# The second mixture's first layer on the byte remainders of the products' operands

## The chip, the cores and the metric

The kernel runs on one core of one Trainium2 chip. The metric is the device time of one execution in microseconds (us); smaller is better. Five engines of the core work side by side, each through its own list of instructions: TensorE (PE, with its weight loads shown apart as PEld), VectorE (DVE), ScalarE (ACT), GpSimd (POOL) and SyncE (SP), which issues most DMAs.

## The reference

Three stages follow each other: linear attention, a mixture of experts with 32 soft slots, and a second mixture that sends every token through all eight experts, weighted by a gate that eight rounds of normalization have balanced. The last takes most of the time, and only it is shown here:

```
def _moe2_ref(x, w_gate, w1, w2):          # x: 2304 tokens x 512
    logits = x @ w_gate
    P = np.exp(logits - logits.max())
    for _ in range(8):
        P /= P.sum(1, keepdims=True) + 1e-09
        P /= P.sum(0, keepdims=True) + 1e-09
        P *= N / E
    for e in range(E):                     # 8 experts, F = 1024
        h = np.maximum(x @ w1[e], 0.0)
        out += P[:, e:e + 1] * (h @ w2[e])
```

The x of this stage is a softmax over 32 slots times the 32 slot outputs, so x @ w1[e] is a product over 32 slots, split in high and low parts to 128 rows.

## The kernel before

**The second mixture.** The 2304 tokens are 9 blocks of 256, and the loop at the end of the kernel runs over 8 experts times 9 blocks, 72 blocks in all, numbered i. For a block, `first_layer(i, n)` makes one half (n = 0, 1) of the hidden layer: four matmuls with a stationary operand of 128x128 from the expert's *stack* (tile st) and the 256 columns of `ct` as moving operand, written to the PSUM tile z. Both operands are fp32r. `ct` holds the softmax over the slots (tiles ct0 to ct3 and ct4, each for two blocks, ct4 for the last block).

**The products.** `hidden(i)` turns z into seven pairs of tiles hh and hl (the rounded high part of a ReLU or of a sum of ReLUs, and what is left of it), made by ACT, DVE and POOL. `product(i, k)`, k = 0 to 6, multiplies a pair by the expert's second-layer weights in a product scheme of seven instead of eight: twelve matmuls each, hh or hl as stationary operand, 256 columns of a weight tile (in the trace w_b or w_t, by the name of its part) as moving one, summed in one of the PSUM tiles x, y, z. `take(i, k)` adds the sum, times the gate, to the output tile xo, on DVE. (Note that z names two PSUM tiles: z<-ct,st is the first layer, z<-w_b a product.)

**The order on PE.** In a block the products come as x (k = 0), z, x; then the first layer of the next block, eight matmuls; then y (k = 3), x, y, x. So 84 product matmuls and 8 of the first layer make a block. All of these have one shape, 128x128 weights and 256 columns. The order is written out by hand; line 51 of the profile is the helper that records every instruction.

**What cuts the stream of matmuls.** When an expert is at its last block, `make_stack` (tile ps) and `spread_stack` (tile pr, from st and the constant rep) make the next expert's stack, between products. In the first expert the normalization of the gate (`sinkhorn`) sums over tokens with a small matmul (tile pcs) once in each of eight rounds, right ahead of the third product.

**Where tiles lie.** Each pool stacks its tiles in the order in which they are first asked for, from its start upward. The pool `const` starts at byte 16512 of each partition and holds, before the change, ct4 (1024 bytes a partition), ident and ones (512 each), wg (128), si (2048), six tiles x0 to x5 (2048 each, later used for ct0 to ct3 and rep) and a tile `pad` of 32 bytes. The pool behind it starts where `const` ends. In the second mixture's pool `cp`, gst (32 bytes) is followed by st (4096) and gm (which takes 32). A byte remainder is the address modulo 512.

Of the kernel before, what the change touches and what calls it, by code (L numbers as in the profile page):

```python
# [7 lines left out]
F32 = mybir.dt.float32  # L8
# [10 lines left out]
E, SPE, FF = 8, 4, 1024  # L19
NS = E * SPE  # L20
KC = DM // 128
# [5 lines left out]
def parts_of(t):  # L27

    out, n = [], t * 128
    while n < (t + 1) * 128:  # L30
        b = n // S
        end = min((b + 1) * S, (t + 1) * 128)
        out.append((b, n - t * 128, end - t * 128))
        n = end
    return out
# [19 lines left out]
def tile_kernel(ctx: ExitStack, tc: tile.TileContext, a):  # L55
# [3 lines left out]
    const = ctx.enter_context(tc.tile_pool(name="const", bufs=1, side="left"))  # L59
# [8 lines left out]
    def load_const(name, shape, pool=None, q=SP):  # L68
        t = (pool or const).tile(shape, F32, name=name, bufs=1)
        q.dma_start(out=t, in_=a[name])  # L70
        return t
# [16 lines left out]
    def w1_unit(name, e, n):  # L88
        return unit_t[name, e, n].rearrange("p (k f) -> p k f", k=2)
# [27 lines left out]
    def load_k(t):  # L117
        x = kp.tile([128, 512], F32, tag="kt", name=f"kt{t}", bufs=4)
        SP.dma_start(out=x, in_=a["kT"][t])
        kt_t[t] = x  # L120

    def load_v(i):
        rows = kp.tile([128, DM], F32, tag="vs", name=f"vs{i}", bufs=2)
        SP.dma_start(out=rows, in_=a["vb"][i])
        x = kp.tile([128, H, XW], F32, tag="vt", name=f"vt{i}", bufs=2)
        G.tensor_copy(out=x[:, :, 0:D], in_=rows.rearrange("p (h d) -> p h d", h=H))
        t, b = VBLOCKS[i]
        parts = parts_of(t)
        for b1, r0, r1 in parts:
            G.memset(x[r0:r1, :, D:XW], float(b1 == b))  # L130
        vt_t[i] = x
# [248 lines left out]
    load_v(0)  # L380
    load_k(2)
    load_v(1)
    ct4 = const.tile([128, 256], F32R, name="ct4", bufs=1)
    ident = load_const("ident", [128, 128])
    ones = load_const("ones", [128, 128])
# [1 line left out]
    for j in range(2):  # L387
        SP.dma_start(out=phi[j * D:(j + 1) * D], in_=a["bd"][j * D:(j + 1) * D, :, j * 96 + D:(j + 1) * 96])
    sel4 = first.tile([128, 128], F32, name="sel4", bufs=1)
    wg = const.tile([128, KC, E], F32, name="wg", bufs=1)  # L390
    lg = early.tile([128, NT, NS], F32, name="lg")
    si = const.tile([128, DM], F32, tag="si", name="si", bufs=1)
    cs = first.tile([128, 2], F32, name="cs")
# [101 lines left out]
            wk = wk_cm.__enter__()  # L495
            attn_units |= {i + 1 + n: (wk, 15 + n) for n in range(7)}
    G = InOrder(tc, G)
    const.tile([128, 8], F32, name="pad", bufs=1)
    while si_steps:
        si_step()  # L500

# [217 lines left out]
    cp = ctx.enter_context(tc.tile_pool(name="cp", bufs=1, side="right", reuse_waits="tile"))  # L719
# [9 lines left out]
    def z_tile(n, name):  # L729
        return pz.tile([128, 1024], F32, tag=f"z{n}", name=name)  # L730

    def make_stack(e):

        ps = z_tile(0, f"ps{e}")[:, 0:256]
        for kc in range(KC):
            w = w1_unit("moe2_w1", e, kc // 2)
            for g in range(4):
                PE.matmul(ps[32 * g:32 * g + 32, :], sot[:, kc, 0:NS], w[:, kc % 2, g * 256:(g + 1) * 256], start=kc == 0, stop=kc == KC - 1)
        for n in range(2):
            unit_t.pop(("moe2_w1", e, n))  # L740

        st = cp.tile([128, FF], F32R, tag="st", name=f"st{e}", bufs=1)
        hl = st[:, FF // 2:].rearrange("p (n f) -> p n f", n=2)
        V.tensor_copy(out=hl[:, 0, :], in_=ps)
        V.tensor_tensor(out=hl[:, 1, :], in0=ps, in1=hl[:, 0, :].bitcast(F32), op=ALU.subtract)
        return st
# [205 lines left out]
    blocks = [(e, blk) for e in range(E) for blk in range(NBLK)]  # L952
    sink = sinkhorn()
    gst = cp.tile([128, E], F32R, name="gst")
    stacks = {0: make_stack(0)}
    gmt = cp.tile([128, 2], F32, name="gm")
    next(sink)
    for k in (4, 5, 6):
        w_part(0, k)
# [108 lines left out]
```

## Time and profile before

| what | us |
|---|---|
| median of 3 runs | 1010.85 |
| the runs | 1010.77 to 1012.33 |
| the profiled execution, its span from first to last instruction | 1010.7 |
| PE busy | 993.3 |
| DVE busy | 691.1 |
| POOL busy | 596.0 |
| ACT busy | 551.8 |

The profiled execution's own time is known as its span; between that and the median of the runs lie 0.15 us. The loop over the 72 blocks begins at about 223 us; what is ahead of it are attention and the first mixture. An engine's busy time is the union of its records. The matmuls' records overlap, each lasting over twice the distance between two starts, so a busy PE says that it never stops, not how quick it is; that is seen from the starts in the timeline.

### The profile page before, as it was taken

What the parts mean: (1) busy time and instruction counts of PE and PEld (TensorE: products, weight loads), DVE (VectorE), ACT (ScalarE), POOL (GpSimd) and SP (SyncE); (2) the same over time, 40 slices, a digit from 0 to 9 for tenths busy, and PEclk for the clock granted to TensorE, in tenths of its full rate; (3) what the DMA queues carried; (4) which work ended last, traced back from release to release, by engine and by line L of the source; (5) the groups of instructions that cost most, each with busy time, mean ns of one, the idle gap of its engine ahead of it and who ended that gap; (6) DMA issues with size and microseconds to landing.
All of it is one profiled execution on the core that took longest, in us unless ns stands there. A gap on an engine that the chain in (4) does not pass through costs nothing.

```text
span 1010.7 us, 27875 instructions
## 1 busy us (share of the span) xinstructions
PE 993.3 (98%) x11638; PEld 938.6 (93%) x11638; DVE 691.1 (68%) x1408; ACT 551.8 (55%) x993; POOL 596.0 (59%) x446
## 2 busy tenths in 40 slices
PE   8999999989999999999999999999999999999998
PEld 7888887449999999999999999999999999999998
DVE  6778876317887677677667676676676677666675
ACT  5665654245566666655565556455555555565442
POOL 2101000475667677858785878578767777686443
PEclk9999999999999999999999999999999999999999
DMA  7767568982003100310031004000400130001111
GB/s 212 227 191 219 162 193 302 350 355 81 1 1 126 43 2 1 126 43 2 2 125 43 2 1 166 3 2 7 161 2 1 65 104 2 1 1 43 43 45 61
DMA packets 25341, 88.84 MB, mean 88 GB/s; under 512 B 3456, under 2 KB 6400, under 8 KB 19328
## 3 DMA queue, kind: packets, MB, share of 16 engines
q1 hardware_dynamic: 19840, 68.05, 19.2%
q10 hardware_dynamic: 5184, 18.88, 6.0%
q8 instruction: 92, 1.51, 0.6%
q14 instruction: 33, 0.27, 0.1%
q0 software_dynamic: 192, 0.13, 0.1%
HBM read 82.33 MB, written 4.72 MB: 86 GB/s over the span
## 4 chain that ended last, share of the span: by engine, by line
PE 95%; DVE 2%; DMA 1%; issue 1%; ACT 1%; DVEq 0%; ACTq 0%
PE x L51 39%; PE y L51 19%; PE z L51 16%; PE kvacc L51 3%; PE num L51 3%; PE pq L51 2%; PE ut L51 2%; PE pk L51 2%; PE ps L51 1%; DMA moe_w<-in_moe_w 1%; PE ph L51 1%; PE po L51 1%; PE lg L51 1%; PE xt L51 1%; PE xl L51 1%
## 5 line engine op out<-in xcount | busy, mean ns | idle before, releaser
L51 POOL TENSOR_TENSOR hl_s<-s,hh_s 128x512 fp32r<-128x512 f32 x286 | 365.5, 1300 | 211.8 <-ACT hh_s L51 192.7
L51 PE MATMUL x<-w_t,hh_s 128*128 128x256 f32 x1152 | 205.4, 278 | 0.0
L51 ACT ACTIVATE hh_s<-s 128x512 fp32r<-128x512 f32 x287 | 175.3, 630 | 52.8 <-DVE s L51 50.4
L51 ACT ACTIVATE r<-z 128x512 f32<-128x512 f32 x143 | 85.6, 599 | 166.5 <-PE z L51 166.0
L51 PEld LDWEIGHTS x<-w_t,hh_s 128*128 128x128 f32 x1152 | 173.7, 188 | 0.8
L51 DVE SCALAR_TENSOR_TENSOR xo<-x,P,xo 128x256 f32<-128x256 f32 x252 | 120.8, 480 | 71.3 <-PE x L51 71.2
L51 ACT ACTIVATE hh_a<-z 128x512 fp32r<-128x512 f32 x216 | 122.3, 600 | 74.4 <-DVE s L51 72.6
L51 PE MATMUL x<-w_t,hl_s 128*128 128x256 f32 x576 | 159.5, 278 | 0.0
L51 DVE SCALAR_TENSOR_TENSOR s<-z,r 128x512 f32<-128x512 f32 x143 | 98.1, 686 | 87.2 <-ACT hh_a L51 82.5
L51 DVE SCALAR_TENSOR_TENSOR hl_a<-z,hh_a 128x512 fp32r<-128x512 f32 x216 | 147.0, 680 | 3.9 <-ACT rt L51 3.9
L51 PEld LDWEIGHTS x<-w_t,hl_s 128*128 128x128 f32 x576 | 108.1, 188 | 0.0
L51 PE MATMUL y<-w_t,hh_s 128*128 128x256 f32 x576 | 103.2, 279 | 0.0
L51 PE MATMUL z<-w_b,hh_a 128*128 128x256 f32 x576 | 102.6, 279 | 0.0
L51 PE MATMUL y<-w_b,hh_s 128*128 128x256 f32 x576 | 102.0, 277 | 0.0
L51 PE MATMUL x<-w_t,hh_a 128*128 128x256 f32 x576 | 102.0, 277 | 0.0
L51 PE MATMUL x<-w_b,hh_a 128*128 128x256 f32 x576 | 101.6, 277 | 0.0
L51 DVE SCALAR_TENSOR_TENSOR s<-z,s 128x512 f32<-128x512 f32 x143 | 97.7, 683 | 3.5 <-POOL hl_s L51 1.3
L51 PEld LDWEIGHTS z<-w_b,hh_a 128*128 128x128 f32 x576 | 86.8, 188 | 2.9 <-issue 2.9
L51 PEld LDWEIGHTS y<-w_t,hh_s 128*128 128x128 f32 x576 | 87.5, 188 | 0.0
L51 PEld LDWEIGHTS x<-w_t,hh_a 128*128 128x128 f32 x576 | 86.9, 188 | 0.1
L51 PEld LDWEIGHTS y<-w_b,hh_s 128*128 128x128 f32 x576 | 86.9, 188 | 0.0
L51 PEld LDWEIGHTS x<-w_b,hh_a 128*128 128x128 f32 x576 | 86.7, 188 | 0.0
(176 smaller groups left out, 1984.5 us busy)
## 6 DMA issues: line engine op xcount, KB each, us to landing
moe_w<-in_moe_w SPq DMA_DIRECT2D x46, 1024.0 KB, 6.0
moe_w<-in_moe_w ACTq DMA_DIRECT2D x36, 512.0 KB, 4.1
vs<-in_vb SPq DMA_DIRECT2D x20, 256.0 KB, 4.0
kt<-in_kT SPq DMA_DIRECT2D x18, 256.0 KB, 3.8
qt<-in_qT SPq DMA_DIRECT2D x18, 256.0 KB, 3.4
out<-xo SPq DMA_DIRECT2D x18, 128.0 KB, 1.7
out<-xo SPq DMA_DIRECT2D x9, 256.0 KB, 2.0
wbd<-in_wbd SPq DMA_DIRECT2D x1, 128.0 KB, 2.7
```

The costliest lines, as they stand in the source:

```text
L51: return lambda *args, **kwargs: self.tc.keep_in_program_order(make(*args, **kwargs))
```

## The change

Tiles are asked for in another order, so that they get other addresses. The built program has the same instructions in the same order on every engine, with the same waits; the order of the instructions shows no difference but the running numbers in the tiles' names.

```
     load_v(1)
+    const.tile([128, 8], F32, name="pad", bufs=1)
+    wg = const.tile([128, KC, E], F32, name="wg", bufs=1)
     ct4 = const.tile([128, 256], F32R, name="ct4", bufs=1)
     ident = load_const("ident", [128, 128])
     ones = load_const("ones", [128, 128])
...
     sel4 = first.tile([128, 128], F32, name="sel4", bufs=1)
-    wg = const.tile([128, KC, E], F32, name="wg", bufs=1)
     lg = early.tile([128, NT, NS], F32, name="lg")
...
     G = InOrder(tc, G)
-    const.tile([128, 8], F32, name="pad", bufs=1)
     while si_steps:
...
     gst = cp.tile([128, E], F32R, name="gst")
+    gmt = cp.tile([128, 2], F32, name="gm")
     stacks = {0: make_stack(0)}
-    gmt = cp.tile([128, 2], F32, name="gm")
     next(sink)
```

What lies ahead of ct4, ident and ones grows by 160 bytes (pad and wg), what lies ahead of si and the x tiles by 32 (pad), what lies ahead of st by 32 (gm). The pools' ends stay where they were, and so do all tiles that aren't listed here:

| tile | its part in matmuls | remainder by 512 before | after |
|---|---|---|---|
| ct0 to ct3 | moving, first layer, blocks 0 to 7 | 256 | 288 |
| ct4 | moving, first layer, block 8 | 128 | 288 |
| st | stationary, first layer; moving for pr | 320 | 352 |
| rep | stationary for pr | 256 | 288 |
| sot | stationary for ps and pgate | 256 | 288 |
| wg | moving for pgate | 128 | 160 |
| ident | moving of all transposes | 128 | 288 |
| ones | stationary for pcs | 128 | 288 |
| si, os, x0 to x5 | in attention and the first mixture | 256 | 288 |
| weight tiles w | moving, all products | 288 | 288 |
| hh, hl | stationary, all products | 352 | 352 |

A matmul of the first layer or of a product steps through its tile by whole multiples of 512 bytes, so that the remainder is that of every such operand.

## Rows read from the trace of the kernel before

**Rows 1.** View of the cores: span us, mean granted TensorE clock.
```profile
core 0: 1010.7 us, clock 1.000
```

**Rows 2.** The page, part 1: busy us, share of the span, instructions.
```profile
PE 993.3 (98%) x11638; PEld 938.6 (93%) x11638; DVE 691.1 (68%) x1408; ACT 551.8 (55%) x993; POOL 596.0 (59%) x446
```

**Rows 3.** The page, part 4: chain that ended last, shares by engine.
```profile
PE 95%; DVE 2%; DMA 1%; issue 1%; ACT 1%; DVEq 0%; ACTq 0%
```

**Rows 4.** Timeline of PE, one block: start us, us, engine, line, operation, tiles.
```profile
589.11 1.10 PE L51 MATMUL z<-ct,st 128*128 128x256 f32 x8
...
590.05 0.41 PE L51 MATMUL y<-w_t,hh_s 128*128 128x256 f32 x2
...
591.43 0.39 PE L51 MATMUL x<-w_t,hh_s 128*128 128x256 f32 x2
...
598.24 0.39 PE L51 MATMUL x<-w_t,hh_s 128*128 128x256 f32 x2
...
599.60 1.11 PE L51 MATMUL z<-ct,st 128*128 128x256 f32 x8
```

**Rows 5.** Groups of PE by form: count, busy us, mean ns, idle before.
```profile
L51 PE MATMUL z<-ct,st 128*128 128x256 f32 x576 | 79.5, 281 | 0.0
...
L51 PE MATMUL x<-w_b,hh_a 128*128 128x256 f32 x576 | 101.6, 277 | 0.0
```

**Rows 6.** Timeline of PE around a new expert's stack.
```profile
609.65 0.28 PE L51 MATMUL z<-w_b,hl_a 128*128 128x256 f32 x1
...
610.71 0.28 PE L51 MATMUL z<-w_b,hl_a 128*128 128x256 f32 x1
...
612.05 0.28 PE L51 MATMUL x<-w_t,hl_s 128*128 128x256 f32 x1
...
612.73 0.28 PE L51 MATMUL x<-w_t,hl_s 128*128 128x256 f32 x1
```

**Rows 7.** Timeline of PE in the last expert.
```profile
919.69 0.28 PE L51 MATMUL y<-w_b,hl_s 128*128 128x256 f32 x1
...
919.86 0.47 PE L51 MATMUL x<-w_t,hh_a 128*128 128x256 f32 x2
...
920.17 0.28 PE L51 MATMUL x<-w_t,hl_a 128*128 128x256 f32 x1
...
921.23 0.28 PE L51 MATMUL x<-w_t,hl_a 128*128 128x256 f32 x1
...
968.92 1.10 PE L51 MATMUL z<-ct,st 128*128 128x256 f32 x8
...
979.75 1.10 PE L51 MATMUL z<-ct,st 128*128 128x256 f32 x8
```

**Rows 8.** Timeline of PE behind three pcs in the first expert.
```profile
241.40 0.28 PE L51 MATMUL x<-w_t,hl_s 128*128 128x256 f32 x1
...
242.58 0.28 PE L51 MATMUL z<-ct,st 128*128 128x256 f32 x1
...
263.44 0.39 PE L51 MATMUL x<-w_t,hh_s 128*128 128x256 f32 x2
...
264.12 0.28 PE L51 MATMUL z<-ct,st 128*128 128x256 f32 x1
...
295.24 0.28 PE L51 MATMUL x<-w_t,hl_s 128*128 128x256 f32 x1
...
296.43 0.28 PE L51 MATMUL z<-ct,st 128*128 128x256 f32 x1
```

**Rows 9.** Groups of PE by form, the transposes of ut.
```profile
L51 PE MATMUL ut<-ident,uq 128*128 128x128 f32 x144 | 21.0, 281 | 1.8 <-DVE x L51 0.6
```

**Rows 10.** Timeline of PE at the loop's start.
```profile
224.37 1.17 PE L51 MATMUL plog<-gst,ct 128*128 128x256 f32 x9
...
225.38 0.52 PE L51 MATMUL x<-w_b,hh_a 128*128 128x256 f32 x3
```

**Rows 11.** Who waited for whom: us in total, times, longest us.
```profile
ACT r L51 <- PE z L51: 166.0, 65, 4.0
```

More of the change, by code (lines that the diff above doesn't have):

```diff
@@ L382, in tile_kernel @@
     load_v(1)
+    const.tile([128, 8], F32, name="pad", bufs=1)
+    wg = const.tile([128, KC, E], F32, name="wg", bufs=1)
     ct4 = const.tile([128, 256], F32R, name="ct4", bufs=1)
@@ L389, in tile_kernel @@
     sel4 = first.tile([128, 128], F32, name="sel4", bufs=1)
-    wg = const.tile([128, KC, E], F32, name="wg", bufs=1)
     lg = early.tile([128, NT, NS], F32, name="lg")
@@ L497, in tile_kernel @@
     G = InOrder(tc, G)
-    const.tile([128, 8], F32, name="pad", bufs=1)
     while si_steps:
@@ L954, in tile_kernel @@
     gst = cp.tile([128, E], F32R, name="gst")
+    gmt = cp.tile([128, 2], F32, name="gm")
     stacks = {0: make_stack(0)}
-    gmt = cp.tile([128, 2], F32, name="gm")
     next(sink)
```

## The prediction

> **What bounds the kernel now.** I began with the view of the cores [rows 1]: one core, 1010.7 us from its first to its last instruction, TensorE's granted clock 1.000, which is the 2.4 GHz level, throughout. So no clock can be won or lost unless an engine stops. The page's busy shares [rows 2] come next: PE is busy 98% of the span, DVE 68%, POOL 59%, ACT 55%. A busy PE is not yet the bound, since its records overlap; the chain that ended last [rows 3] says that it is: 95% of it lies on PE. What counts is therefore not how long one matmul lasts but how far apart two successive ones start, its pace, and that is read from the timeline.
>
> [Rows 4] show one block of the second mixture. Sixty product matmuls start between 591.43 and 598.24 us: 6.81 us, or 113.5 ns each. The eight first-layer matmuls ahead of them take from 589.11 to 590.05 us: 0.94 us, or 117.5 ns each, for the same shape (128x128 weights, 256 columns, fp32r). And the product right behind them, y, takes from 590.05 to 591.43 us, 1.38 us for twelve, where twelve at 113.5 ns are 1.36. So a block has two dear places: the first layer (0.94 against 8 x 0.1135 = 0.91 us) and the first matmuls behind it (0.02 us). From one first layer to the next, 589.11 to 599.60 us, are 10.49 us; 92 matmuls (84 of products, 8 of the first layer) at 113.5 ns are 10.44 us. The groups [rows 5] say that this is no single case: over all 576 first-layer matmuls one record lasts 281 ns, over 576 product matmuls of one kind 277 ns.
>
> The trace shows one more thing that the forecast must reckon with: the slower pace also occurs with the products' own operands. After the gap that a new expert's stack makes, nine matmuls start between 609.65 and 610.71 us, 118 ns each, while behind the next gap six start between 612.05 and 612.73 us, 113 ns each [rows 6]. In the last expert a small stall (0.17 us between two starts, at 919.69 us) throws the stream to the slower pace, nine matmuls from 920.17 to 921.23 us, 118 ns each, and it stays there to the end: 968.92 to 979.75 us, 10.83 us for a block [rows 7]. So the stream has two paces, about 113 and 118 ns, and it can be kicked from the one to the other.
>
> **The change, part by part.** No instruction is added, removed or moved, and no wait changes. Addresses alone change: the first layer's moving operand (ct) goes from remainder 256 (128 for the last block of each expert) to 288, its stationary operand (the stack) from 320 to 352, where the products' operands lie. ident, ones, si, x, sot and rep also get remainder 288, wg 160.
>
> *First layer.* What would it cost with the products' remainders? From below: its pace might not move at all (nothing, if addresses aren't the cause). From above: it takes the products' pace, 113.5 ns, and the y behind it loses its 0.02 us: 10.49 - 10.44 = 0.05 us a block. I take the upper end, because the products, with this shape and these types, differ from the first layer in little but addresses, and because entering and leaving the first layer is what breaks their even pace in [rows 4]. It holds for the blocks in which the stream is at the quicker pace when the first layer comes: the second block to the last of the seventh expert, 9 x 7 = 63. The blocks of the last expert, but for its first, run at the slower pace anyway [rows 7], with products as slow as first layer, so nothing is won there. 63 x 0.05 = 3.2 us.
>
> *The first expert.* Eight times the column sums (pcs) of the normalization cut the stream here. Behind four of these cuts the product stays slow: the first is 241.40 to 242.58 us, ten matmuls at 118 ns, the last 295.24 to 296.43 us; behind the other four it returns to 113 ns within a few matmuls, as 263.44 to 264.12 us, six matmuls [rows 8]. In the kernel before, the pace is quick again soon behind the next first layer. If the first layer no longer differs from its surroundings, nothing there may end the slow pace, and it could last to the next cut, a block later. A block at the slow pace is 10.83 us against 10.49 now, 0.34 us; four of them with the gain that they then miss, 4 x (0.34 + 0.05) = 1.6 us, less what of it is slow already: 1.4 us at most, nothing at least. No row decides between the ends, so I take the middle, 0.7 us.
>
> *The transposes and the small products.* ident is the moving operand of the transposes ahead of the second mixture, 144 of them ut's [rows 9] and some 276 in all. If ident's new place gave them the 4.5 ns that part the two paces, that would be 1.2 us; a gain as large is the other end. Their moving operand has 128 columns, half of the first layer's, and PE waits a little ahead of them as it is (1.8 us ahead of ut's). I take nothing. ps, pr, pgate and sot are a dozen kinds of matmul that run once per expert or once: nothing, as are the loads of wg and rep, which nothing waits for.
>
> *Other engines.* They write ct and the stack, and st's neighbour gm, at other addresses, the same lengths and partitions. Bound: nothing either way, since they wait for PE by far more than the 0.05 us in question: ACT for z alone 65 times, 166.0 us [rows 11]. What is late next if PE gains 0.05 us a block: whatever made PE wait at 919.69 us [rows 7], the one such stall behind the first expert; that place would come a little earlier and wait a little longer, with the same end.
>
> **Sum.** 3.2 - 0.7 = 2.5 us. The profiled execution has 1010.7 us as its own span, 0.15 below the median of the runs, 1010.85; so the forecast is 1010.85 - 2.5 = 1008.3 us after rounding down.
>
> **A rule weighed.** [Rows 4] give 117.5 ns for the first layer, 113.5 ns for products, with like shapes. The Trainium skill, TensorE: Matmul & The Clock Gate, section "Part 2: What happens when you issue a matmul", has two independent SBUF read ports on PE, so that loading the next weights takes nothing from the running matmul's reads; and SBUF — State Buffer, "Door 1: The DMA port swizzle", knows lines of 16 bytes, in which remainders 256, 288, 320 and 352 are all alike. By these two the change could do nothing, 1010.85 us; the trace's two paces for one shape aren't explained by them.
>
> **Rivals.**
> (a) *Addresses aren't the cause.* The first layer also differs in that every matmul starts and ends its own sum and writes new PSUM columns. Against it: the router's plog matmuls do that too, and nine of them start between 224.37 and 225.38 us, 112 ns each [rows 10]. (Their moving operand is 8 columns read over and over, so it is no clean comparison.) For it: products run at 118 ns as well [rows 6, 7], with the good addresses. Time: 1010.85 us.
> (b) *The slow pace sticks* — the case on the other side. With one address pattern all through, what the gap ahead of an expert leaves behind stays. The matmuls of pr, which close that gap, read the moved stack and rep; their timing decides in which pace x resumes. Now it resumes quick [rows 6]. If it resumed slow, the expert's blocks would cost 0.34 us more each, as in the last expert [rows 7], with no first layer to end it: for six experts 54 x 0.34 = 18.4 us, and 1010.85 + 18.4 = 1029 us. It decides from one expert on: 9 x 0.39 = 3.5 us is more than the 2.5 of the sum. Against it: the quick pace came back behind this gap in every expert, with x's own addresses, which don't change.
> (c) *The last expert gets the quick pace too*, because the stall at 919.69 us falls away or leaves the stream otherwise: about 8 blocks of 10.83 - 10.44 = 0.39 us, another 3.1 us: 1005.2 us.
> (d) *Given back elsewhere*: the first expert's 1.4 us in full and the transposes' 1.2 us: 3.2 - 2.6 = 0.6 us, 1010.2 us.
>
> **How the numbers follow.** The forecast 0.54, (a) 0.16, (b) 0.14, (c) 0.08, (d) 0.08. The forecast's own range is 1007.2 us (none of the 0.7 paid, and a little from the transposes) to 1009.1 us (all 1.4 paid). The range for all: from (c), 1005.0, to just over no change, 1011.1 us; outside are (b) and part of (a) and (c). A measurement of this kernel tells 0.2%, 2.0 us, from no change: below 1008.8 us is faster. Of the forecast 0.50 lies there, with (c) 0.58. The same: (a), (d) and 0.04 of the forecast, 0.28. Slower: (b), 0.14.
>
> **What would show it.** In the profile after: the group of the first layer at 277 ns instead of 281; a first layer in the timeline of about 0.91 us, the y behind it 1.36 us, a block 10.44 us in the second to seventh expert. If those blocks stay 10.49 us, (a) is right. Blocks of 10.83 us from an expert's start are (b), in the first expert the 1.4 us. A last expert with blocks of 10.44 us is (c). The transposes' groups, ut at 281 ns, should not move. The forecast is wrong if the first layer gets quicker while the span doesn't fall by a like sum.

## The result, and the profile after

The change made the kernel slower: a median of 1017.32 us (1014.47 to 1019.46, five runs) against 1011.25 us (1010.77 to 1012.85, five runs) of the kernel before on the same chip. The ratio is 1.0052, with a 95% interval of 1.0036 to 1.0068. Forecast were 1008.3 us and a range of 1005.0 to 1011.1. Five executions are left out of the ratios below as slow ones: the profiled one of run 9 (granted clock 0.753; its trace isn't read), one each of runs 4 and 18 (0.789 and 0.753), and one each of runs 9 and 16 (1036.57 and 1033.40 us, at 0.996 and 1.000).

The cores, part 1 of the page, and three groups of PE by form after the change (count, busy us, mean ns, idle before), to be held against [rows 1, 2, 5, 9]:

```profile
core 0: 1012.7 us, clock 1.000
```
```profile
PE 995.1 (98%) x11638; PEld 940.1 (93%) x11638; DVE 691.0 (68%) x1408; ACT 551.4 (54%) x993; POOL 595.8 (59%) x446
```
```profile
L51 PE MATMUL x<-w_b,hh_a 128*128 128x256 f32 x576 | 102.2, 278 | 0.0
...
L51 PE MATMUL z<-ct,st 128*128 128x256 f32 x576 | 77.8, 278 | 0.0
...
L51 PE MATMUL ut<-ident,uq 128*128 128x128 f32 x144 | 21.1, 281 | 1.7 <-DVE x L51 0.6
```

The first layer did get quicker, 278 ns instead of 281, while the products' group went from 277 to 278, the transposes stayed, and the span grew by 2.0 us. The timeline of PE after the change (start us, us, engine, line, operation, tiles) shows both sides: the cut by pr ahead of the third expert, at 417.56 us, the same cut ahead of the fifth, at 614.33 us, and behind it an even block:

```profile
417.56 0.51 PE L51 MATMUL pr<-st,rep 32*128 32x256 f32 x8
...
418.34 0.28 PE L51 MATMUL x<-w_t,hl_s 128*128 128x256 f32 x1
...
419.40 0.28 PE L51 MATMUL x<-w_t,hl_s 128*128 128x256 f32 x1
419.52 1.11 PE L51 MATMUL z<-ct,st 128*128 128x256 f32 x8
420.46 0.40 PE L51 MATMUL y<-w_t,hh_s 128*128 128x256 f32 x2
...
614.33 0.51 PE L51 MATMUL pr<-st,rep 32*128 32x256 f32 x8
...
615.46 0.28 PE L51 MATMUL x<-w_t,hl_s 128*128 128x256 f32 x1
...
616.14 0.28 PE L51 MATMUL x<-w_t,hl_s 128*128 128x256 f32 x1
...
626.68 1.07 PE L51 MATMUL z<-ct,st 128*128 128x256 f32 x8
627.59 0.39 PE L51 MATMUL y<-w_t,hh_s 128*128 128x256 f32 x2
...
628.95 0.39 PE L51 MATMUL x<-w_t,hh_s 128*128 128x256 f32 x2
...
637.11 1.07 PE L51 MATMUL z<-ct,st 128*128 128x256 f32 x8
```

In the even block the first layer takes 0.91 us (626.68 to 627.59), y behind it 1.36 us (to 628.95), the block 10.43 us (to 637.11), against 0.94, 1.38 and 10.49 of [rows 4]. That is the forecast gain. But behind the cut at 417.56 us the stream resumes at the slow pace: nine matmuls from 418.34 to 419.40 us, 118 ns each, and the first layer takes 0.94 us (419.52 to 420.46), with the same addresses. Behind the like cut at 614.33 us six take 0.68 us, 113 ns each (615.46 to 616.14).

How long it lasts is seen in the chain that ended last (its longest pieces in order of time: start us, us, what). Two successive products x, 24 matmuls, stand there once a block; 2.72 us are 113.3 ns each, 2.83 us are 117.9:

```profile
248.85 2.83 PE x L51 x24
259.68 2.72 PE x L51 x24
...
411.44 2.72 PE x L51 x24
424.87 2.83 PE x L51 x24
435.70 2.83 PE x L51 x24
...
511.55 2.83 PE x L51 x24
524.79 2.72 PE x L51 x24
...
694.39 2.72 PE x L51 x24
718.25 2.83 PE x L51 x24
...
794.10 2.83 PE x L51 x24
```

All nine blocks of the third expert (424.87 to 511.55 us) and of the sixth (from 718.25 us) are slow, 10.83 us from one to the next (424.87 to 435.70). The next cut ends it. Between the first layers that open them, a quick expert is 96.61 or 96.65 us long, a stuck one 100.12 us; before, an expert was 97.14 us.

The two profiled executions differ so, by the starts of each expert's first layer:

| stretch | before | after | difference |
|---|---|---|---|
| up to the loop's first block | 223.44 | 224.38 | +0.94 |
| first expert | 97.98 | 98.49 | +0.51 |
| second, fourth, fifth, seventh expert, together | 388.58 | 386.52 | -2.06 |
| third and sixth, together | 194.28 | 200.24 | +5.96 |
| last expert to the end | 106.42 | 103.07 | -3.35 |
| sum | | | +2.0 |

The first line need not be the change's: in the profiled executions of all kernels here (without run 9) the loop begins anywhere between 223.3 and 228.8 us, and in two executions of one kernel (runs 5 and 18) at 224.5 and 225.8. In the last, the stall of [rows 7] comes after the change too (0.20 us between two starts, ahead of 925.13 us), but the stream is quick again behind it. Without that the profiled execution would have been 5.4 us slower than before, not 2.0.

### The profile page after: what moved, and what is told of

Same layout as the page of the kernel before. It is cut to its first block, busy times and chain, and to the rows that moved or that the text cites. A ratio compares the mean times of both kernels' runs of the same rounds, so it can differ in the third digit from the quotient of the medians.

```text
span 1012.7 us, 27875 instructions
## 1 busy us (share of the span) xinstructions
PE 995.1 (98%) x11638; PEld 940.1 (93%) x11638; DVE 691.0 (68%) x1408; ACT 551.4 (54%) x993; POOL 595.8 (59%) x446
## 4 chain that ended last, share of the span: by engine, by line
PE 95%; DVE 2%; DMA 1%; ACT 1%; issue 1%; DVEq 0%; ACTq 0%
PE x L51 39%; PE y L51 19%; PE z L51 16%; PE kvacc L51 3%; PE num L51 3%; PE pq L51 2%; PE ut L51 2%; PE pk L51 2%; PE ps L51 1%; DMA moe_w<-in_moe_w 1%; PE ph L51 1%; PE po L51 1%; PE lg L51 1%; PE xt L51 1%; PE xl L51 1%
```

## The experiments

Two theories. **Theory 1**: a first layer with other remainders than the products' is what ends a slow pace; with like remainders the pace that a cut leaves is kept. **Theory 2**: the operands of the matmuls that close a cut (pr, and pcs in the first expert) decide at which pace the stream resumes; the first layer is innocent.

Every run is compared with the kernel before on its own chip (medians of before 1010.8 us for runs 1 to 4, 1012.75 for 5 to 8, 1011.75 for 9 to 12, 1011.0 for 13 to 16, 1010.62 for 17 and 18). "Slow experts" counts those that run at 10.83 or 10.84 us a block from their cut on, of the six that only a stack cuts off (third to eighth; the second expert's cut is closed by the last pcs, not by pr); "slow blocks" those of 11.0 us and more among the six blocks of the first expert from its third on. Remainders are streamed/held. The span is that of the profiled execution.

| run | first layer | pr | pcs | ratio to before | span | slow experts | slow blocks |
|---|---|---|---|---|---|---|---|
| before | 256/320 | 320/256 | 448/128 | 1 | 1010.7 | 0 | 0 |
| change | 288/352 | 352/288 | 448/288 | 1.0052 [1.0036, 1.0068] | 1012.7 | 2 | 3 |
| 1 | 288/320 | 320/288 | 448/288 | 1.0113 [1.0096, 1.0129] | 1025.5 | 3 | 3 |
| 2 | 256/352 | 352/256 | 448/128 | 1.0190 [1.0175, 1.0205] | 1028.7 | 6 | 6 |
| 3 | 224/288 | 288/224 | 448/224 | 1.0033 [1.0018, 1.0047] | 1010.6 | 0 | 4 |
| 4 | 288/352, two blocks 256/352 | 352/288 | 448/288 | 1.0065 [1.0039, 1.0090] | 1014.7 | 2 | 3 |
| 5 | 288/352 | 320/256 | 448/288 | 0.9976 [0.9960, 0.9993] | 1010.6 | 0 | 3 |
| 6 | 256/320 | 352/288 | 448/128 | 1.0044 [1.0018, 1.0070] | 1013.2 | 0 | 0 |
| 7 | 256/320 | 320/256 | 448/128 | 1.0001 [0.9985, 1.0017] | 1011.4 | 0 | 0 |
| 8 | 288/352 | 288/224 | 448/288 | 0.9989 [0.9973, 1.0005] | 1005.9 | 0 | 3 |
| 9 | 288/352 | 288/224 | 448/128 | 1.0043 [1.0019, 1.0067] | | | |
| 10 | 288/352 | 352/256 | 448/288 | 1.0107 [1.0088, 1.0127] | 1020.6 | 3 | 3 |
| 11 | 288/352 | 320/288 | 448/288 | 1.0095 [1.0077, 1.0113] | 1019.2 | 3 | 3 |
| 12 | 256/320 | 320/288 | 448/128 | 1.0100 [1.0076, 1.0124] | 1018.1 | 3 | 0 |
| 13 | 288/352 | 352/352 | 448/288 | 1.0177 [1.0162, 1.0192] | 1027.2 | 6 | 3 |
| 14 | 288/352 | 288/352 | 448/288 | 1.0073 [1.0051, 1.0094] | 1017.8 | 2 | 3 |
| 15 | 288/352 | 448/384 | 448/288 | 0.9999 [0.9984, 1.0014] | 1008.0 | 0 | 3 |
| 16 | 288/352 | 288/224 | 448/128 | 1.0022 [1.0009, 1.0035] | 1010.4 | 0 | 6 |
| 17 | 288/352 | 288/224 | 448/384 | 0.9993 [0.9981, 1.0005] | 1008.3 | 0 | 6 |
| 18 | 288/352 | 320/256 | 448/288 | 0.9969 [0.9957, 0.9980] | 1007.2 | 0 | 3 |

**Runs 1 to 4: one part alone, both elsewhere, two blocks old.** The edits to the change, one after the other:

```
run 1  stacks = {0: make_stack(0)}
      +gmt = cp.tile([128, 2], F32, name="gm")      # behind st again
run 2 -const.tile([128, 8], F32, name="pad")        # pad and wg back
      -wg = const.tile([128, KC, E], F32, name="wg")
run 3 -const.tile([128, 8], F32, name="pad")
      +const.tile([128, 120], F32, name="pad")
      +const.tile([128, 16], F32, name="padb")      # at the end of const
      +cp.tile([128, 16], F32, name="padc")         # behind st; cp, whose end is fixed, begins 64 bytes lower
run 4 +const.tile([128, 120], F32, name="pada")     # ahead of the tile of ct0
      +const.tile([128, 8], F32, name="padb")       # behind it
```

Run 1: 

> The change with the stack left at remainder 320; the first layer's moving operand, rep, ones and ident are moved as in the change. Theory 1 (the slow pace sticks because the first layer no longer differs from its surroundings, in either operand): the first layer stays at about 0.94 us and is followed by the quick pace, no expert from the second to the seventh runs at 10.83 us a block, time within 2 us of the kernel before. If it is the moving operand alone that counts: first layer 0.91 us, some whole experts at 10.83 us, 1014 to 1019 us, as the change. Theory 2 (the moved operands of the matmuls that cut the stream, rep and ones, draw the pace, and the first layer is innocent): some whole experts at 10.83 us although the first layer is at 0.94 us.

Run 2: 

> Only the stack is moved, to 352; everything in the constants lies as before. Theory 1: if the stationary operand alone counts, the first layer takes 0.91 us and some whole experts stick at 10.83 us a block, 1013 to 1019 us; if the moving operand or both count, first layer 0.94 us, quick pace behind it, 1010 to 1012 us. Theory 2: rep, ones and ident lie as before, so no expert sticks, whatever the first layer takes; 1007 to 1012 us.

Run 3: 

> The change with both operands of the first layer 64 bytes lower, ct at 224 and the stack at 288, the products' operands as they are at 288 and 352. If only the remainder by 64 counts (32 in both): as the change, first layer 0.91 us in quick stretches, some experts at 10.83 us a block, 1013 to 1019 us. If the place by 512 counts: first layer about 0.94 us and no sticking expert from the second to the seventh, 1010 to 1012 us.

Run 4: 

> The change, but ct0, the moving operand of the first two blocks of every expert, stays at remainder 256; all others at 288, the stack at 352. Theory 1: these two first layers (0.94 us, if the moving operand counts) bring the stream back to the quick pace behind every expert's cut, and the other seven take 0.91 us: no sticking expert from the second to the seventh, 54 blocks at about 0.05 us less, 2 to 3 us under the kernel before but for what the first expert's cuts cost (up to 1.5 us): 1008 to 1010 us. Theory 2: some experts stick all the same, 1013 to 1019 us.

The groups of the first layer in runs 1, 2 and 3, in this order, to be held against 278 ns in the change and 281 before:

```profile
L51 PE MATMUL z<-ct,st 128*128 128x256 f32 x576 | 79.7, 281 | 0.0
```
```profile
L51 PE MATMUL z<-ct,st 128*128 128x256 f32 x576 | 79.8, 281 | 0.0
```
```profile
L51 PE MATMUL z<-ct,st 128*128 128x256 f32 x576 | 79.9, 282 | 0.0
```

First, the gain needs both operands: in quick blocks a first layer at 288/320 takes 117.9 ns a matmul, at 256/352 117.4, at 224/288 118.5 (the block is 10.48 us); only at 288/352 it takes 113.4. Second, Theory 1 has experts recover wherever the first layer differs; in run 1 three of six run slow from their cut to the next, and in run 2 all six from their cut to the first layer of their last block, which reads ct4 (128/352) and is followed by the quick pace. In run 4 the third and the sixth stick as in the change, although their first two first layers differ. In run 3, where both lie 64 bytes lower, none sticks, but nothing is gained either. That leaves what pr reads, which had moved in all four. Theory 2 as put down ahead of run 2 failed as well: it counted rep and ones, which lie as before there, and not the stack, which pr streams.

**Runs 5 to 8: pr by itself.** The parts that pr streams get a tile apart, so that the first layer and pr can be placed one without the other. Run 5 is the change with pr as before, run 6 is before with pr as in the change, run 7 is before with the tile apart and nothing else, run 8 the change with pr 64 bytes lower.

```
-hl = st[:, FF // 2:].rearrange("p (n f) -> p n f", n=2)
+hl = const.tile([128, DM + 128], F32R, tag="x5", name=f"hl{e}")[:, off:off + DM]
-rep = const.tile([128, 512], F32R, tag="x4", name="rep")[:, 0:256]
+rep = const.tile([128, 512], F32R, tag="x4", name="rep")[:, off2:off2 + 256]
```

Run 5: 

> The change, but the product pr behind each expert's cut reads the byte remainders it had before (320 for the streamed columns, 256 for the held ones), from a tile apart; the first layer keeps 288 and 352. Theory 2 (the cutting product's own operands decide the pace that the stream resumes at, whatever the first layer reads): no expert from the third on is slow throughout, quick blocks stay at 10.43 us, the time is 1007 to 1010 us. Theory 1 (a first layer with unequal remainders ends the slow pace, one with equal remainders keeps it): experts still stick at 10.8 us a block, 1014 to 1019 us as the change.

Run 6: 

> The kernel before, but pr reads the remainders of the change (352 and 288); the first layer keeps 256 and 320. Theory 2: some of the later experts are slow throughout (3.1 us each), 1013 to 1020 us. Theory 1: the first layer ends every slow pace within a block, 1010 to 1012 us.

Run 7: 

> Control for the two others: the kernel before with the high and low parts of the stack in the tile apart, at the same remainders (320 and 256) as before. Both theories: within 0.2% of before, 1010 to 1012 us. If it is off by more, the place of the tile and not its remainder counts.

Run 8: 

> The change, but pr reads 288 (streamed) and 224 (held), as in the run that lay 64 bytes lower, where no later expert was slow; the first layer keeps 288 and 352. Theory 2: no later expert sticks, quick blocks 10.43 us, 1007 to 1010 us, faster than before. Theory 1: 1014 to 1019 us.

Behind a stack Theory 2 holds. With pr's old operands the change is faster than before, with the change's operands before is slower, and the tile apart costs nothing. In the profiled execution of run 6 no expert stuck from its cut, so there the loss in its other runs has only the times for it. Run 8 missed its forecast of a gain: no expert sticks in its profile and quick blocks are 10.43 us, yet its ratio, 0.9989, can't be told from 1. So it is with runs 15 and 17 below; what their other executions lost has no trace. Of the pairs tried, 320/256 (runs 5 and 18) alone gave a gain clear of noise.

A new stall comes with the quick blocks: wherever the sixth expert ran at 10.43 us a block (runs 5, 8, 11, 14 to 18), its fifth block took 10.53 to 10.58 us, with 0.19 or 0.20 us between two starts, which before doesn't have. In runs 5 and 11 the stream is slow from there to the expert's end (98.25 and 98.24 us); the column "slow experts" doesn't count these two.

**Runs 9 to 12: which operand.** Run 10 puts only rep back (off2 = 120), run 11 only hl (off = 8), run 12 is before with rep alone 32 bytes further on (off2 = 8). Run 9 is run 8 with the weights of pcs at their old 128, by a copy (x4 is the tile of rep, made 640 wide):

```
+ones2 = x4[:, 472:472 + 128]
+G.tensor_copy(out=ones2, in_=ones)
-PE.matmul(pg[:, 0:E], ones, csf, start=True, stop=True)
+PE.matmul(pg[:, 0:E], ones2.bitcast(F32), csf, start=True, stop=True)
```

Run 9: 

> The run with pr at 288 and 224 again, and the weights of the column sums pcs, which cut the stream in the first expert, at their old remainder 128 (a copy of ones). If the cutting product's operands decide there too (Theory 2), the first expert's blocks from the third on are 10.70 to 10.77 us each, without one of 11.03, about 1.0 us less than in the profiled run of the kernel it starts from. If the old first layer (256 and 320) was what ended the slow pace there (Theory 1), three or more of them stay at 11.03 us.

Run 10: 

> The change, with only rep, the held operand of pr, at its old remainder 256; the streamed one at 352. If the held operand is what counts: no expert from the third on sticks, 1007 to 1011 us. If the streamed one counts: some stick, 1014 to 1019 us. If it is the pair, either may come.

Run 11: 

> The change, with only the high and low parts of the stack, the streamed operand of pr, at their old remainder 320 (in a tile apart); rep at 288. If the streamed operand is what counts: no expert from the third on sticks, 1007 to 1011 us. If the held one counts: some stick, 1014 to 1019 us.

Run 12: 

> The kernel before with only rep at 288; everything else where it was. If the held operand of pr is what counts: as the run of before with both of pr's operands moved, 1014 to 1019 us. If it is the streamed one: 1010 to 1013 us.

Neither operand alone is right: runs 10 to 12 are all worse than the change. Run 12 is the plainest: one constant moved by 32 bytes, no instruction changed, costs 1.0% (the interval is 0.8 to 1.2%). Its chain, as above:

```profile
411.77 2.72 PE x L51 x24
425.20 2.83 PE x L51 x24
...
511.86 2.83 PE x L51 x24
525.19 2.72 PE x L51 x24
...
609.07 2.72 PE x L51 x24
622.50 2.83 PE x L51 x24
...
709.16 2.83 PE x L51 x24
722.49 2.72 PE x L51 x24
```

The pace changes at every cut: third expert slow, fourth quick, fifth slow, sixth quick. A cut that the stream reaches quick leaves it slow, one that it reaches slow leaves it quick. So it is in runs 1, 10 and 11 too. The timeline shows why: a cut has two halves, ps and pr, with the product z between them. Here it is at the cuts ahead of the third and of the fourth expert:

```profile
416.63 0.28 PE L51 MATMUL z<-w_b,hl_a 128*128 128x256 f32 x1
...
417.69 0.28 PE L51 MATMUL z<-w_b,hl_a 128*128 128x256 f32 x1
...
418.68 0.28 PE L51 MATMUL x<-w_t,hl_s 128*128 128x256 f32 x1
...
419.74 0.28 PE L51 MATMUL x<-w_t,hl_s 128*128 128x256 f32 x1
...
516.82 0.28 PE L51 MATMUL z<-w_b,hl_a 128*128 128x256 f32 x1
...
517.85 0.28 PE L51 MATMUL z<-w_b,hl_a 128*128 128x256 f32 x1
```

Behind a quick stream, z is slow (nine matmuls from 416.63 to 417.69 us, 118 ns each), and so is x behind pr (418.68 to 419.74). Behind a slow one, z is quick (nine from 516.82 to 517.85, 114 ns each), and x too. So it is ps that turns the pace over, and pr here leaves it as it is; in [rows 6] pr with its old operands lifts a slow z to a quick x. In all 114 cuts of the third to the eighth expert (19 traces, without run 9's) z ends at the other pace than the stream had ahead of ps, whatever remainder sot had (224, 256 or 288). Behind pr the pace is that of z in 30 of 30 cuts of runs 1, 2 and 10 to 12.

The medians of runs 1, 2 and 10 to 13 (1020.8 to 1029.7 us) lie above every range that was put down ahead of them. In run 12 the first layer has its old remainders, 256/320, through all of the slow experts: Theory 1 falls for the experts behind a stack, with these remainders at least (ct4's 128/352 in run 2 did end the slow pace).

**Runs 13 to 16: is it the difference?** The three pairs that never stick (320/256, 288/224, and by run 15 448/384) have the streamed operand 64 bytes above the held one. Run 13 has the two alike (off 16, off2 16), run 14 exchanged (0, 16), run 15 both 96 higher than the change (40, 24). Run 16 is run 9 once more.

Run 13: 

> The change, with both operands of pr at 352 (no difference between them). If a difference of 64 bytes between the streamed and the held operand is what makes the stream resume quick: later experts stick, 1014 to 1024 us, in the profiled run two or more of the seven. If any pair does that keeps clear of 288 for the held one: 1007 to 1011 us.

Run 14: 

> The change, with pr's operands exchanged: 288 for the streamed, 352 for the held (as the first layer and the products have them). By the difference (here 64 the other way round): some stick, 1014 to 1024 us. If operands that lie like those of the products behind them make the stream go on evenly: none sticks, 1007 to 1011 us.

Run 15: 

> The change, with pr at 448 (streamed) and 384 (held): a difference of 64 at another place. By the difference: no expert is slow from its cut on, 1007 to 1013 us on a chip where before has 1010 to 1013 us. If the places themselves count: some stick, 1014 us and more.

Run 16: 

> The kernel with pr at 288 and 224 and the weights of pcs at 128, once more, since its profiled run had a granted clock of 0.753. Theory 2 for the first expert (the cutting product's operands decide): blocks of 10.70 to 10.77 us from the third on, none of 11.03. Theory 1 for the first expert (only the old first layer, 256 and 320, ends the slow pace there): three or more of 11.03 us. The time says which later places are slow when it is again 1014 us and more.

With a difference of 64 at these three places none of 54 cuts left an expert slow (six in each of before and runs 3, 5, 7, 8, 15, 16, 17, 18), although z was slow in 52 of them; with 0, 32, 96 or -64, 26 of 42 did (runs 1, 2, 10 to 14). In run 13 it is every expert from the third on, by its chain:

```profile
424.88 2.83 PE x L51 x24
...
525.06 2.83 PE x L51 x24
...
725.43 2.83 PE x L51 x24
...
925.80 2.83 PE x L51 x24
```

But the change's own pair, 352/288, has a difference of 64 as well and left 4 of 18 slow (2 in its profile, 2 in run 4, none in run 6). So the difference sorts these runs, and is not the whole rule.

Run 16 shows the first expert, by its chain:

```profile
237.54 2.83 PE x L51 x24
...
303.90 2.83 PE x L51 x24
...
416.10 2.82 PE x L51 x24
429.35 2.72 PE x L51 x24
```

With pcs reading its old 448/128 all blocks there are slow, 11.06 us. With the same pcs and the old first layer (before, runs 6, 7, 12) none is. In before the product right behind the pcs at 240.95 us is slow as well (241.40 to 242.58 us of [rows 8]), but the two x behind the next first layer are quick, by its chain:

```profile
247.79 2.72 PE x L51 x24
```

So in the first expert Theory 1 is the better one: the old first layer brought the quick pace back. But not any first layer that differs does: 256/352 (run 2) leaves six blocks slow, 224/288 (run 3) four, 288/320 (run 1) three. The second expert is slow in run 16 too and ends with the x at 416.10 us. Its cut is closed by the last pcs:

```profile
321.14 0.51 PE L51 MATMUL pr<-hl,rep 32*128 32x256 f32 x8
322.33 0.39 PE L51 MATMUL pcs<-cs,rep 128*128 128x8 f32 x2 [0.68 <-ACT st L51]
```

**Runs 17 and 18: pcs by the difference, and the best pair again.** Run 17 is run 16 with the copy at `x4[:, 408:408 + 128]`, run 18 is run 5 once more.

Run 17: 

> The change with pr at 288 and 224 and the weights of pcs at 384, which makes the difference of 64 bytes to its streamed operand at 448, too. If the difference of 64 is a rule for any cutting product: the first expert's blocks from the third on are all 10.70 us, 1.0 us below the runs where three are 11.03, and the time is below before, 1004 to 1010 us. If pcs follows no such rule: some of them stay at 11.03 us or more, and the first expert hands a slow pace on in some executions.

Run 18: 

> The change with pr at 320 and 256 again, on another chip and in more rounds, to see whether its ratio of 0.9976 to before holds. Theory 2: 0.996 to 0.999, no expert from the second on slow from its cut on. If the first ratio was chance: 0.999 to 1.002.

In run 17 the first expert's blocks are 11.06 us, all six: the difference of 64 is no rule for pcs. Run 18 holds what run 5 gave: the change with pr where it was is 0.31% faster than before (the interval is 0.2 to 0.4%), median 1008.45 us against 1010.62. Its chain, with slow blocks in the first expert alone:

```profile
304.49 2.83 PE x L51 x24
315.33 2.72 PE x L51 x24
...
412.91 2.72 PE x L51 x24
...
715.94 2.72 PE x L51 x24
```

Against the profiled execution of before, its second to seventh experts save 3.1 us together and its last one 3.3 (it is quick behind the stall), while the first takes 0.5 longer and the loop begins 2.4 later. In how many of the other executions the last expert is quick isn't known, so the times don't tell how much of the 0.31% is the first layer's gain.

## Why the prediction was wrong

*The first layer* (0.94 to 0.91 us, y 1.38 to 1.36 us) was right: a block that runs at the quick pace is 10.43 us, 0.06 less than before, and runs 1 to 3 show that it takes both operands where the products have them. Rival (a), that addresses aren't the cause, is out.

*The step that failed* is the one on the small products, "ps, pr, pgate and sot are a dozen kinds of matmul that run once per expert or once: nothing", and with it the answer to rival (b), that the quick pace would come back behind pr "with x's own addresses, which don't change". Of pr only its own eight matmuls were counted; in the profiled execution what the stream does behind them cost 7.0 us, two experts at 3.51 us more than a quick one. Rival (b) had named that pr reads the moved tiles, and the mechanism (pr's operands decide the pace that x resumes in) and the price (3.5 us for an expert) were right; only its chance, 0.14, was taken from the kernel before, in which pr had read other addresses. Run 5 (pr put back, 0.9976) and run 12 (rep alone, 1.0100) show what decides. Rival (b) also took the missing difference of the first layer for what lets the slow pace stay; run 12 shows that behind pr the old first layer doesn't end it either. And it took the pace that "came back behind this gap" for x's own; but [rows 6] have z at 118 ns behind ps and x at 113 behind pr, and by run 12 it is pr, with its old operands, that brought the quick pace back.

*The first expert*: 0.7 us was taken, 0 to 1.4 the bounds. It came out 0.51 us longer, by three blocks of 11.03 us against 10.77. The sum had also counted a gain of 9 x 0.05 = 0.45 us there, so in its terms the loss was 0.96 us. In its place and cause it was right, as run 16 against before shows.

*Other engines*: one stall behind the first expert was foreseen; the sixth expert's, above, is a second one.

*The last expert*: rival (c) came in the profiled execution, -3.35 us. That is luck, and no effect of the change alone: behind the same stall run 7, which reads what before reads, is quick, and run 5, which keeps the change's first layer, is slow. Which it is in a given execution stays open.

*The sum*: the profiled execution's own time was put 0.15 us from the median. The runs here lie some 1.8 us above their spans (1014.47 with 1012.7), so that of before was likely the longest of its three, 1012.33 us, with the slow last expert in it. In place of 2.5 us gained, 6.1 were lost in the medians. The profile accounts for the stuck experts, two in it; the change's other four runs were 1.4 to 5.0 us longer than the profiled one, which one more stuck expert (3.5 us) or a slow last one (3.3 us) could make in part, but they have no trace. With pr where it was, the gain is 2.4 us (0.0024 x 1012.75, run 5) and 3.1 us (0.0031 x 1010.62, run 18), about the forecast of 2.5.

*A rule weighed*: the Trainium skill, TensorE: Matmul & The Clock Gate, "Part 2: What happens when you issue a matmul", has two independent read ports for the running matmul and the next weights, and SBUF — State Buffer, "Door 1: The DMA port swizzle", has lines of 16 bytes; by neither is one remainder here better than another. Run 12 differs (1.0100 for 32 bytes), and the measurement decides.

Open stay: why ps turns the pace over, and why the pair of remainders of pr decides whether that is undone; why 352/288 sticks in some cuts and not in others; what pcs would have to read; which first layers end a slow pace, and why 256/320 does behind pcs and not behind pr; and which way the stream goes behind the stall in the last expert.

## What to carry to other kernels

When addresses are changed for the operations that a stream is made of, the operations that interrupt it and read the same tiles move too; count what the stream does behind them, over all the time to the next interruption, and not their own duration. A recovery seen in the trace of before is evidence only as long as all that takes part in it reads the same places. Try such a move with the interrupting operations kept where they are, as in run 18, before it is dropped.

## What was not expected of the hardware

At a granted clock of 1.000 the same matmul (128x128 weights, 256 columns, fp32r) runs in two even paces, 113.3 and 117.8 ns from start to start, and a stream of over 700 of them keeps the one that it was left in for 86 us, until the next interruption (424.87 to 511.55 us above, 736 matmuls). One interruption, ps, turned the pace over in 114 of 114 cuts; eight matmuls of pr, some 0.4 us of work, decide whether that is undone, by where their two operands lie. 32 bytes on one of them cost 3.0 us for every expert left slow in run 12 (100.13 us against 97.15 before), and 3.5 in run 11 against run 5 (100.13 against 96.61). A cut can even change the pace each time (run 12), so that the loss depends on what came before it.
